# Query features of a fused attention kernel from a second, transposed projection instead of transposed copies

## The chip, the cores and the metric

The kernel runs on one core of a Trainium2 chip, in one launch. The time is device microseconds of that core. Its engines work side by side, each through its own instructions in order: TensorE (PE, with PEld for its weight loads), VectorE (DVE), ScalarE (ACT), GpSimd (POOL), and SyncE (SP), which issues the transfers. Matrix products land in PSUM; the attention turns over six banks of it for all tiles but kv.

## The reference, cut to what matters

Random-feature attention over 4 batches, 8 heads, 576 positions and 64 dimensions with 128 features, and then a mixture of experts on its output (2304 tokens, 512 wide, 8 experts). The change touches `q_p` alone.

```python
def phi(x):
    proj = np.einsum('bhsd,md->bhsm', x, omega)
    sq = np.sum(x * x, axis=-1, keepdims=True) / 2.0
    h = proj - sq
    h = h - np.max(h, axis=-1, keepdims=True)
    return np.exp(h) / np.sqrt(m)
q_p, k_p = (phi(q_s), phi(k_s))
kv = np.einsum('bhsm,bhsd->bhmd', k_p, v)
z = np.sum(k_p, axis=2)
num = np.einsum('bhsm,bhmd->bhsd', q_p, kv)
den = np.einsum('bhsm,bhm->bhs', q_p, z)[..., None] + 1e-06
```

Everything here is fp32. For one position the squared norm and the maximum are the same for all 128 features, so they form one shift per position and head, which is added ahead of the exponential.

## The kernel before

The attention is cut into 36 jobs, 18 of keys and 18 of queries; a job is 128 positions of eight (head, position) slots, kept as two groups g of four. `tick(j)` runs once for each job and overlaps several: for job j it makes the projection (`projections`, tile pp, two banks), the maxima (`maxima`), the shift (`shifts`, tile cn) and the exponentials (`exps`, tile ex); for job j+2 it transposes the input (tile tp, copied to th); for job j-1 it multiplies keys by values (`keys_by_values`, tile kv) or turns the query features; for job j-2 it multiplies query features by that product (`numerators`, tile np) and divides (`quotients`, tile xt). Ticks 5 to 29 take key and query jobs mostly in turn, the last six take queries only.

The features of a query job come out of `exps` with positions on the partitions. `numerators` needs them as stationary operand with features on the partitions. So `query_transposes` sends them through TensorE eight times (tile qp) and `query_copy` brings them back to SBUF on ScalarE (tile qt), one tick after their exponential.

In `projections` and `numerators` the operands cover half of the array: a projection has 64 rows, and the two groups g stand in the upper and the lower half.

The order on each engine is that of the code: the attention's instructions are chained one behind the other in the list `pinned`. Among the ticks `go_on` also advances the work that prepares the experts: sums on GpSimd, casts on ScalarE (tiles wh, xs) and subtractions on VectorE (wl, xs). The experts' products (tiles hx, hz, x, z) follow the attention and fill the rest of the span.

Of the kernel before, what the change touches and what calls it, by code (L numbers as in the profile page):

```python
# [9 lines left out]
F32 = mybir.dt.float32  # L10
F32R = mybir.dt.float32r
AF = mybir.ActivationFunctionType
ALU = mybir.AluOpType
# [9 lines left out]
def moe_attention_kernel(  # L23
# [306 lines left out]
    omt = sc.tile([P, M], F32, name="omt")  # L330

# [113 lines left out]
    def transposed_copy(jb):  # L445

        which, tp = jb[0], tps.pop(jb)
        th = sc.tile([P, 4, P], F32, tag="th", bufs=2, name="th")
        if which == "k":
            nc.scalar.copy(th.rearrange("p a s -> p (a s)"), tp)  # L450
        else:
            nc.vector.tensor_copy(th.rearrange("p a s -> p (a s)"), tp)
        ths[jb] = th

    def projections(jb):

        th = ths.pop(jb)
# [16 lines left out]
    def shifts(jb):  # L474

        cn = sc.tile([P, 8], F32, tag="cn", bufs=4, name="cn")
        nc.vector.tensor_reduce(cn, shift_of(jb), axis=AX.X, op=ALU.add)
        ex = [sc.tile([P, 4, M], F32, tag="ex", bufs=6, name="ex") for _ in range(2)]
        nc.vector.tensor_tensor(
            ex[0], p3s[jb][0], cn[:, 0::2].unsqueeze(2).to_broadcast([P, 4, M]), op=ALU.add  # L480
        )
        cns[jb], exs[jb] = cn, ex

    def exps(jb, g):

        ex = exs[jb][g]
# [7 lines left out]
    tps, ths, p3s, cns, exs, qts, nums = {}, {}, {}, {}, {}, {}, {}  # L494
# [57 lines left out]
    def query_transposes(jb):  # L552

        ex = exs.pop(jb)
        tps = []
        for g in (1, 0):
            tp = bank("qp")
            for i in range(4):
                nc.tensor.transpose(tp[:, i * P : (i + 1) * P], ex[g][:, i, :], ident)
            tps.append((g, tp))  # L560
        return tps

    def query_copy(jb, g, tp):

        t = sc.tile([P, 4, P], F32, tag="qt", bufs=4, name="qt")
        nc.scalar.copy(t.rearrange("p a s -> p (a s)"), tp)
        qts[jb, g] = t
# [443 lines left out]
    def tick(j):  # L1011
# [25 lines left out]
        close()  # L1037
        if now:
# [17 lines left out]
        if job(j - 1, "q"):  # L1056
            for t in query_transposes(job(j - 1)):
                query_copy(job(j - 1), *t)
# [9 lines left out]
        if now:  # L1068
            if it:
                next(it)  # L1070
            exps(now, 1)
        go_on()
# [3 lines left out]
        if now:  # L1076
            exps(now, 0)
# [34 lines left out]
    z = len(jobs)  # L1112
    numerators(jobs[z - 2])
    for g, tp in query_transposes(jobs[z - 1]):
        query_copy(jobs[z - 1], g, tp)
# [143 lines left out]
```

## Time and profile before

| | |
|---|---|
| median of 3 runs | 1576.74 us (1575.73 to 1577.12) |
| the profiled execution | 1575.99 us, of which the span is 1574.2 us |
| TensorE busy | 1561.7 us, 99% of the span |
| TensorE weight loads | 1535.4 us, 98% |
| VectorE, ScalarE, GpSimd busy | 1361.5, 766.2, 277.1 us |
| granted TensorE clock | full speed in all 40 slices |

Attention takes about the first 147 us; the experts take the rest. A matrix product in fp32 stands in the trace as two records (eight projections of a job are 16 MATMUL records), a transpose as one. Ends of matmuls are modelled, so what a group of them takes is read from its start to the start of the next group. That way is used below.

### The profile page before, as it was taken

How to read it: one execution, taken by the hardware profiler on the slowest of the kernel's cores; microseconds unless marked ns; L12 is line 12 of the kernel's file. 1: busy time of each engine (PE TensorE's matmuls, PEld its weight loads, DVE VectorE, ACT ScalarE, POOL GpSimd, SP SyncE). 2: the span in 40 equal slices, each digit the busy share in tenths (PEclk: the TensorE clock that was granted, in tenths of full speed). 3: DMA queues.
4: the chain of work that ended last, by engine and by line, in shares of the span. 5: the costliest groups of instructions: out<-in, count | busy, mean ns of one | idle time of the engine just before them, and what ended most of it. 6: DMA issues, size and time to landing. Idle time of an engine off the chain costs nothing.

```text
span 1574.2 us, 31256 instructions
## 1 busy us (share of the span) xinstructions
PE 1561.7 (99%) x12295; PEld 1535.4 (98%) x12295; DVE 1361.5 (86%) x2573; ACT 766.2 (49%) x1388; POOL 277.1 (18%) x285
## 2 busy tenths in 40 slices
PE   9999999999999999999999999999999999999999
PEld 8887999999999999999999999999999999999998
DVE  7999989898888898888789898889888888989775
ACT  8998654444443444444444443444443444444341
POOL 6665211111010111111011111111110111110000
PEclk9999999999999999999999999999999999999999
DMA  9546866645666666656666666656566666656562
GB/s 227 139 148 259 332 249 223 229 173 214 210 222 215 225 197 216 222 176 216 214 221 212 225 208 212 217 185 225 195 219 212 216 217 208 225 185 212 182 230 92
DMA packets 105730, 330.81 MB, mean 210 GB/s; under 512 B 14704, under 2 KB 43888, under 8 KB 105584
## 3 DMA queue, kind: packets, MB, share of 16 engines
q1 hardware_dynamic: 105296, 328.55, 61.8%
q8 instruction: 98, 1.61, 0.4%
q14 instruction: 48, 0.39, 0.1%
q10 hardware_dynamic: 288, 0.26, 0.0%
HBM read 307.54 MB, written 21.23 MB: 209 GB/s over the span
## 4 chain that ended last, share of the span: by engine, by line
PE 91%; DVE 3%; DMA 3%; ACT 1%; SPq 1%; POOL 1%; issue 0%; DVEq 0%; POOLq 0%; ACTq 0%
PE hx L730 25%; PE x L854 25%; PE hz L730 19%; PE z L854 19%; PE p L938 1%; PE pp L462 1%; DMA xd<-xs 1%; DVE sqs L472 1%; DMA oa<-xd 1%; DMA xs<-xd 1%; DMA k<-in_k_dram 1%; DVE xs L125 0%; PE tp L442 0%; PE np L583 0%; PE kv L499 0%
## 5 line engine op out<-in xcount | busy, mean ns | idle before, releaser
L730 PE MATMUL hx<-xs,wh 128*128 128x384 f32 x1528 | 367.0, 335 | 1.1 <-ACT hn L745 0.8
L730 PE MATMUL hz<-xs,wh 128*128 128x384 f32 x1144 | 282.1, 336 | 0.3 <-DMA xs<-xd 0.3
L730 PEld LDWEIGHTS hx<-xs,wh 128*128 128x128 f32 x1528 | 265.4, 188 | 2.8 <-ACT xs L120 1.4
L235 POOL TENSOR_TENSOR st<-st 128x512 f32<-128x512 f32 x75 | 117.6, 1568 | 613.6 <-DVE wl L269 611.3
L828 ACT ACTIVATE bh<-hr 128x512 fp32r<-128x512 f32 x141 | 89.1, 632 | 237.6 <-PE x L854 230.1
L730 PEld LDWEIGHTS hz<-xs,wh 128*128 128x128 f32 x1144 | 199.8, 188 | 1.5 <-DVE out L888 0.9
L730 PE MATMUL hx<-xs,wl 128*128 128x384 f32 x764 | 200.1, 335 | 0.0
L888 DVE SCALAR_TENSOR_TENSOR out<-x,prob,out 128x256 f32<-128x256 f32 x324 | 153.7, 477 | 52.3 <-PE x L854 50.4
L268 ACT CAST wh<-st 128x512 fp32r<-128x512 f32 x172 | 103.5, 620 | 103.4 <-PE hx L730 52.1
L730 PE MATMUL hz<-xs,wl 128*128 128x384 f32 x572 | 151.8, 335 | 0.0
L825 DVE TENSOR_TENSOR sl<-sm,sh 128x512 fp32r<-128x512 f32 x141 | 112.7, 799 | 44.2 <-ACT sh L823 38.4
L823 ACT CAST sh<-sm 128x512 fp32r<-128x512 f32 x141 | 87.7, 622 | 106.3 <-PE z L854 82.0
L730 PEld LDWEIGHTS hx<-xs,wl 128*128 128x128 f32 x764 | 137.4, 188 | 0.0
L269 DVE TENSOR_TENSOR wl<-st,wh 128x512 fp32r<-128x512 f32 x172 | 123.1, 725 | 9.9 <-ACT wh L268 9.9
L783 DVE SCALAR_TENSOR_TENSOR sm<-hr,sm 128x256 f32<-128x256 f32 x282 | 124.6, 442 | 3.0
L809 ACT CAST sh<-sm 128x512 fp32r<-128x512 f32 x140 | 87.1, 622 | 71.3 <-PE x L854 68.5
L854 PE MATMUL z<-wh,sh 128*128 128x256 f32 x564 | 115.9, 280 | 0.6 <-ACT sh L809 0.5
L854 PE MATMUL x<-wl,sh 128*128 128x256 f32 x564 | 114.5, 280 | 0.0
L854 PE MATMUL z<-wl,sh 128*128 128x256 f32 x564 | 113.9, 280 | 0.0
L854 PE MATMUL x<-wh,sl 128*128 128x256 f32 x564 | 113.6, 279 | 0.0
L791 ACT ACTIVATE ah<-hr 128x256 fp32r<-128x256 f32 x141 | 58.9, 418 | 109.8 <-PE x L854 95.5
L854 PE MATMUL x<-wh,sh 128*128 128x256 f32 x564 | 112.3, 279 | 0.0
(194 smaller groups left out, 3555.6 us busy)
## 6 DMA issues: line engine op xcount, KB each, us to landing
xs<-xd SPq DMA_DIRECT2D x327, 768.0 KB, 4.5
st<-in_moe_w_dram SPq DMA_DIRECT2D x66, 512.0 KB, 4.9
xd<-xs SPq DMA_DIRECT2D x21, 768.0 KB, 5.3
v<-in_v_dram SPq DMA_DIRECT2D x8, 512.0 KB, 7.0
q<-in_q_dram SPq DMA_DIRECT2D x8, 512.0 KB, 7.1
k<-in_k_dram SPq DMA_DIRECT2D x7, 512.0 KB, 7.3
out_dram<-out SPq DMA_DIRECT2D x18, 128.0 KB, 3.9
oa<-xd SPq DMA_DIRECT2D x2, 768.0 KB, 8.9
```

Of the source, the lines that this page charges most:

```text
L235: nc.gpsimd.tensor_tensor(o, a, b, op=op)
L268: nc.scalar.copy(hi, o)
L269: nc.vector.tensor_tensor(lo, o, raw(hi), op=ALU.subtract)
L730: nc.tensor.matmul(pb, lhsT=a[:, k, g * P : (g + 1) * P], rhs=x[:, b, k, :], start=i in (1, 5, 2) and j == 0, stop=j == len(prods) - 1, sk ...
L783: nc.vector.scalar_tensor_tensor(o, in0=a, scalar=0.0, in1=b, op0=ALU.max, op1=op)
L791: nc.scalar.activation(ah, a11, AF.Relu)
L809: nc.scalar.copy(sh, sm)
L823: nc.scalar.copy(sh, sm)
L825: nc.vector.tensor_tensor(sl, sm, raw(sh), op=ALU.subtract)
L828: nc.scalar.activation(bh, a[:, 1:], AF.Relu)
L854: nc.tensor.matmul(pb, lhsT=ops[s][i][a][:, f], rhs=wt[u, 2, i][b][:, f], start=bool(start) and j == 0, stop=j == len(prods) - 1, skip_gro ...
L888: nc.vector.scalar_tensor_tensor(o, in0=pb, scalar=p, in1=o, op0=ALU.mult, op1=ALU.add)
```

## The change

The query job makes no exponential in its own tick. Its shift goes into a zeroed tile cw (`shifts`). In the next tick one transpose on TensorE turns cw, into the job's own first pp bank, and VectorE copies it to a tile ct (`shifts_turned`). `query_features` then projects again with operands exchanged: omega is stationary and the transposed input th moves, 512 columns for each group; eight more products add row i of ct to the 128 columns of slot i, by a stationary operand that repeats one column of the identity. The result is the features' exponent with features on the partitions, and `query_exps` makes two exponentials of 512 columns straight from PSUM into qt. The eight transposes, the two copies, the addition of the shift on VectorE and the five exponentials of a query job go. th is kept a tick longer (4 buffers for 2), and qt shares the buffers of ex (7 for 6 and 4).

```diff
@@ -328,6 +328,10 @@
     sc.tile([P, 1, D], F32, name="om2")
     oms = sc.tile([P, 2, D], F32, name="oms")
     omt = sc.tile([P, M], F32, name="omt")
+    wide = [sc.tile([P, P], F32, name=f"cw{i}") for i in range(2)]
+    turnedc = [sc.tile([P, P], F32, name=f"ct{i}") for i in range(2)]
+    for t in wide:
+        nc.gpsimd.memset(t, 0.0)
 
     def busy(n):
 
@@ -445,7 +449,7 @@
     def transposed_copy(jb):
 
         which, tp = jb[0], tps.pop(jb)
-        th = sc.tile([P, 4, P], F32, tag="th", bufs=2, name="th")
+        th = sc.tile([P, 4, P], F32, tag="th", bufs=4, name="th")
         if which == "k":
             nc.scalar.copy(th.rearrange("p a s -> p (a s)"), tp)
         else:
@@ -454,7 +458,7 @@
 
     def projections(jb):
 
-        th = ths.pop(jb)
+        th = ths[jb] if jb[0] == "q" else ths.pop(jb)
         pp = [bank("pp") for _ in range(2)]
         for i in range(4):
             for g in range(2):
@@ -473,9 +477,18 @@
 
     def shifts(jb):
 
+        if jb[0] == "q":
+            cnw = wide[len(cnws) % 2]
+            cnws.append(cnw)
+            nc.vector.tensor_reduce(
+                cnw.rearrange("p (g c) -> p c g", g=2)[:, :4, :],
+                shift_of(jb).rearrange("p (i g) t -> p i g t", g=2),
+                axis=AX.X, op=ALU.add,
+            )
+            return
         cn = sc.tile([P, 8], F32, tag="cn", bufs=4, name="cn")
         nc.vector.tensor_reduce(cn, shift_of(jb), axis=AX.X, op=ALU.add)
-        ex = [sc.tile([P, 4, M], F32, tag="ex", bufs=6, name="ex") for _ in range(2)]
+        ex = [sc.tile([P, 4, M], F32, tag="ex", bufs=7, name="ex") for _ in range(2)]
         nc.vector.tensor_tensor(
             ex[0], p3s[jb][0], cn[:, 0::2].unsqueeze(2).to_broadcast([P, 4, M]), op=ALU.add
         )
@@ -483,6 +496,8 @@
 
     def exps(jb, g):
 
+        if jb[0] == "q":
+            return
         ex = exs[jb][g]
         if g == 0:
             nc.scalar.activation(ex, ex, AF.Exp)
@@ -491,7 +506,7 @@
         for i in range(4):
             nc.scalar.activation(ex[:, i, :], p3s[jb][1][:, i, :], AF.Exp, bias=c4[:, i : i + 1])
 
-    tps, ths, p3s, cns, exs, qts, nums = {}, {}, {}, {}, {}, {}, {}
+    tps, ths, p3s, cns, exs, qts, nums, cts, qps = {}, {}, {}, {}, {}, {}, {}, {}, {}
 
     def kv_mm(b, h, r, ex, rhs, z, start, stop):
 
@@ -549,22 +564,41 @@
     closing = []
     xts = {}
 
-    def query_transposes(jb):
-
-        ex = exs.pop(jb)
-        tps = []
-        for g in (1, 0):
-            tp = bank("qp")
-            for i in range(4):
-                nc.tensor.transpose(tp[:, i * P : (i + 1) * P], ex[g][:, i, :], ident)
-            tps.append((g, tp))
-        return tps
-
-    def query_copy(jb, g, tp):
-
-        t = sc.tile([P, 4, P], F32, tag="qt", bufs=4, name="qt")
-        nc.scalar.copy(t.rearrange("p a s -> p (a s)"), tp)
-        qts[jb, g] = t
+    cnws = []
+
+    def shifts_turned(jb):
+
+        cp = p3s[jb][0].rearrange("p h m -> p (h m)")[:, :P]
+        nc.tensor.transpose(cp, cnws[-1], ident)
+        ct = turnedc[len(cnws) % 2]
+        nc.vector.tensor_copy(ct, cp)
+        cts[jb] = ct
+        p3s.pop(jb)
+
+    def query_features(jb):
+
+        th, ct = ths.pop(jb), cts.pop(jb)
+        qp = [bank("qp") for _ in range(2)]
+        rows = [slice(g * D, (g + 1) * D) for g in range(2)]
+        for g, r in enumerate(rows):
+            nc.tensor.matmul(
+                qp[g][:, :], lhsT=omt[r], rhs=th[r].rearrange("p a s -> p (a s)"), start=True, stop=False,
+                skip_group_check=True,
+            )
+        for i in range(4):
+            for g, r in enumerate(rows):
+                nc.tensor.matmul(
+                    qp[g][:, i * P : (i + 1) * P], lhsT=ident[r, g * D + i : g * D + i + 1].to_broadcast([D, M]),
+                    rhs=ct[r], start=False, stop=i == 3, skip_group_check=True,
+                )
+        qps[jb] = qp
+
+    def query_exps(jb):
+
+        for g, qp in enumerate(qps.pop(jb)):
+            t = sc.tile([P, 4, P], F32, tag="ex", bufs=7, name="qt")
+            nc.scalar.activation(t.rearrange("p a s -> p (a s)"), qp, AF.Exp)
+            qts[jb, g] = t
 
     def numerators(jb):
 
@@ -1035,6 +1069,9 @@
                 kv_copy(*closed[-1])
 
         close()
+        prev = job(j - 1, "q")
+        if prev:
+            shifts_turned(prev)
         if now:
             projections(now)
             maxima(now, 0)
@@ -1053,9 +1090,8 @@
             next(it)
         if 1 <= j < 3:
             ensure_squares(j - (j < 2))
-        if job(j - 1, "q"):
-            for t in query_transposes(job(j - 1)):
-                query_copy(job(j - 1), *t)
+        if prev:
+            query_features(prev)
         if now:
             if not nxt:
                 go_on()
@@ -1069,12 +1105,13 @@
             if it:
                 next(it)
             exps(now, 1)
+            exps(now, 0)
+        if prev:
+            query_exps(prev)
         go_on()
         for xt, i, t in turned[: 1 if j < 28 else None]:
             turned.pop(0)
             token_copy(token_transposes(xt, i, t), t)
-        if now:
-            exps(now, 0)
         for it in leftover:
             next(it, None)
         leftover.clear()
@@ -1110,9 +1147,10 @@
         tick(i)
         ensure_loads(i + 1)
     z = len(jobs)
+    shifts_turned(jobs[z - 1])
     numerators(jobs[z - 2])
-    for g, tp in query_transposes(jobs[z - 1]):
-        query_copy(jobs[z - 1], g, tp)
+    query_features(jobs[z - 1])
+    query_exps(jobs[z - 1])
     go_on()
     xpss = [token_transposes(*it) for it in turned[:2]]
     quotients(jobs[z - 2])
```

On TensorE, a key tick and the query tick behind it (jobs 9 and 10). Before, from the product of keys and values (kv) that ends the tick ahead:

```order
L499 MATMUL kv<-v_94,ex 64x65 x16
L462 MATMUL pp<-omt,th 128x128 x8
L442 MATMUL tp<-ident,k 128x128 x4
L559 MATMUL qp<-ident,ex 128x128 x8
L462 MATMUL pp<-omt,th 128x128 x8
L442 MATMUL tp<-ident,q 128x128 x4
L583 MATMUL np<-kvs,qt 64x65 x16
```

And in the changed kernel:

```order
L514 MATMUL kv<-v_100,ex 64x65 x16
L572 MATMUL pp<-ident,cw_92 128x128
L466 MATMUL pp<-omt,th 128x128 x8
L446 MATMUL tp<-ident,k 128x128 x4
L584 MATMUL qp<-th,omt 128x512 x2
L590 MATMUL qp<-ct_93,ident 128x128 x8
L466 MATMUL pp<-omt,th 128x128 x8
L446 MATMUL tp<-ident,q 128x128 x4
L617 MATMUL np<-kvs,qt 64x65 x16
```

The transpose of cw stands ahead of the key job's projection, and two products of 512 columns and eight of 128 stand where the eight transposes stood.

On ScalarE, in the same two ticks, from the copies of the earlier query job. Before:

```order
L566 COPY qt<-qp 128x512 x2
L450 COPY th<-tp 128x512
L492 ACTIVATE ex<-pp,cn 128x128 x4
L488 ACTIVATE ex<-ex 128x512
L417 ACTIVATE sq<-q 128x1024
L492 ACTIVATE ex<-pp,cn 128x128 x4
L488 ACTIVATE ex<-ex 128x512
```

And in the changed kernel:

```order
L454 COPY th<-tp 128x512
L507 ACTIVATE ex<-pp,cn 128x128 x4
L503 ACTIVATE ex<-ex 128x512
L600 ACTIVATE qt<-qp 128x512 x2
L421 ACTIVATE sq<-q 128x1024
```

What fills qt stood ahead of the key job's exponentials and now stands behind them; the query job's own five exponentials are gone.

On VectorE, over the same two ticks. Before:

```order
L472 TENSOR_REDUCE sqs<-pp 128x4 x2
L477 TENSOR_REDUCE cn<-sqs 128x8
L479 TENSOR_TENSOR ex<-pp,cn 128x512
L514 TENSOR_TENSOR kvs<-kv,kvs 128x4
L472 TENSOR_REDUCE sqs<-pp 128x4 x2
L477 TENSOR_REDUCE cn<-sqs 128x8
L479 TENSOR_TENSOR ex<-pp,cn 128x512
L452 COPY th<-tp 128x512
```

And in the changed kernel:

```order
L574 COPY ct_94<-pp 128x128
L476 TENSOR_REDUCE sqs<-pp 128x4 x2
L490 TENSOR_REDUCE cn<-sqs 128x8
L492 TENSOR_TENSOR ex<-pp,cn 128x512
L529 TENSOR_TENSOR kvs<-kv,kvs 128x4
L476 TENSOR_REDUCE sqs<-pp 128x4 x2
L483 TENSOR_REDUCE cw_92<-sqs 128x4x2
L456 COPY th<-tp 128x512
```

The query job's addition of 512 columns (ex) goes, a copy of 128 columns (ct) comes in, and the small sum writes cw instead of cn. On GpSimd two memsets of 128 columns come in at the program's start. Behind the attention no engine's order changes.

## Rows read from the trace of the kernel before

**Rows 1.** Busy time and instructions of each engine, and shares of the chain, whole span.

```profile
PE 1561.7 (99%) x12295; PEld 1535.4 (98%) x12295; DVE 1361.5 (86%) x2573; ACT 766.2 (49%) x1388; POOL 277.1 (18%) x285
PE 91%; DVE 3%; DMA 3%; ACT 1%; SPq 1%; POOL 1%; issue 0%; DVEq 0%; POOLq 0%; ACTq 0%
```

**Rows 2.** Chain that ended last, by time: start, length (both us), what.

```profile
14.38 8.32 DMA k<-in_k_dram
...
35.88 0.87 PE qp L559 x8
...
64.45 1.07 ACT qt L566 x2
...
85.38 1.11 DVE xs L125
...
129.88 2.36 POOL v L116
```

**Rows 3.** Busy time by stretch: us, each engine's busy time (instructions), granted clock, DMA.

```profile
28.00:64.00 36.00, 36.00 (x596) 32.44 (x593) 32.01 (x76) 32.80 (x82) 21.08 (x43) 1.00 0.85 210
64.00:85.00 21.00, 20.50 (x328) 17.08 (x328) 17.98 (x42) 20.55 (x50) 14.20 (x25) 1.00 0.01 2
85.00:125.00 40.00, 38.62 (x608) 33.52 (x605) 38.67 (x86) 35.02 (x86) 29.02 (x46) 1.00 0.51 167
125.00:147.00 22.00, 20.69 (x323) 16.16 (x322) 20.94 (x53) 19.84 (x42) 18.90 (x11) 1.00 0.59 231
```

**Rows 4.** Timeline of TensorE, jobs 9 and 10: start, length to the modelled end (us).

```profile
34.13 1.16 PE L462 MATMUL pp<-omt,th 64*128 64x128 f32 x16
35.23 0.66 PE L442 MATMUL tp<-ident,k 128*128 128x128 f32 x4
35.72 1.04 PE L559 MATMUL qp<-ident,ex 128*128 128x128 f32 x8
36.69 1.46 PE L462 MATMUL pp<-omt,th 64*128 64x128 f32 x16
38.08 0.65 PE L442 MATMUL tp<-ident,q 128*128 128x128 f32 x4
38.66 1.15 PE L583 MATMUL np<-kvs,qt 128*64 128x65 f32 x32
...
40.68 1.16 PE L462 MATMUL pp<-omt,th 64*128 64x128 f32 x16
```

**Rows 5.** Timeline of TensorE around the gate's logits (lp), and one later projection.

```profile
79.25 1.50 PE L194 MATMUL lp<-xf,wgs 128*32 128x384 f32 x16
80.68 1.16 PE L462 MATMUL pp<-omt,th 64*128 64x128 f32 x16
...
115.90 1.60 PE L462 MATMUL pp<-omt,th 64*128 64x128 f32 x16
```

**Rows 6.** Groups of instructions, 0 to 200 us: busy us, mean ns, idle before.

```profile
L492 ACT ACTIVATE ex<-pp,cn 128x128 f32<-128x128 f32 x144 | 42.8, 417 | 4.7 <-DVE cn L477 4.3
L488 ACT ACTIVATE ex<-ex 128x512 f32<-128x512 f32 x36 | 25.4, 705 | 0.0
L479 DVE TENSOR_TENSOR ex<-pp,cn 128x512 f32<-128x512 f32 x36 | 24.9, 691 | 2.0
L566 ACT COPY qt<-qp 128x512 f32<-128x512 f32 x36 | 20.1, 617 | 5.6 <-PE qp L559 5.5
L602 DVE TENSOR_TENSOR xt<-np,rd 128x256 f32<-128x256 f32 x36 | 13.6, 418 | 0.6
```

**Rows 7.** Timeline of VectorE and then of ScalarE, job 9's way to its exponentials.

```profile
36.80 0.18 DVE L477 TENSOR_REDUCE cn<-sqs 128x8 f32<-128x24 f32 x1
...
37.79 1.17 ACT L492 ACTIVATE ex<-pp,cn 128x128 f32<-128x128 f32 x4
38.80 0.68 ACT L488 ACTIVATE ex<-ex 128x512 f32<-128x512 f32 x1
39.33 1.10 ACT L417 ACTIVATE sq<-q 128x1024 f32<-128x1024 f32 x1
```

**Rows 8.** Timeline of GpSimd at the start of the span.

```profile
0.86 0.20 POOL L87 MEMSET ones<- 128x128 f32 x1
```

## The prediction

> **What bounds the kernel now.** I read the busy times first. TensorE is busy 99% of the span and carries 91% of the chain that ended last [rows 1]; the change touches only the attention, so the question is what bounds the first 147 us. The chain, read by time, gives the stages [rows 2]. Up to 23 us it runs through transfers. From 28 to 64 us it stays on TensorE, group behind group. Then it passes through ScalarE (64 to 85 us), through VectorE (85 to 125 us), and from 130 us through GpSimd and a transfer, until the experts' first products take over. Next I took busy times by these four stages [rows 3]. TensorE has no idle time in the first, 0.5 us in the second, 1.4 us of 40 in the third and 1.3 us of 22 in the last. So where the chain names ScalarE or VectorE, TensorE is nearly full as well, and a longer TensorE program has little room anywhere. The timeline of one key tick and one query tick shows it piece by piece [rows 4]: one group starts where the other ends.
>
> The clock is granted in full in every stage [rows 3], so each price below holds throughout.
>
> **Prices on TensorE.** Start to start [rows 4]: eight projections of 128 columns take 1.10 us (34.13 to 35.23); four transposes take 0.49 us when transposes follow and 0.58 us when products of another shape follow, so a seam between shapes costs 0.09 us; the eight transposes of query features with their seam take 0.97 us, so 0.11 us each. The projection behind them takes 1.39 us. That is 0.29 us longer than 1.10: it stretches while its second bank waits to be emptied.
>
> What each query job costs after the change:
> - The eight transposes go: 8 x 0.11 = 0.88 us less.
> - Eight products of 128 columns and 64 rows come in. They have the shape of the projections, upper and lower half in turn. Of the 1.10 us some 0.2 are the seams at both ends, so 0.90 us.
> - Two products of 512 columns come in, two records each. No row shows this width. A projection's sixteen records take eight turns of the two halves, 0.90 / 8 = 0.11 us for 128 columns; 512 columns make that 0.45 us a turn, and two turns 0.90 us. The gate's logits (384 columns, four turns of four blocks side by side) take 1.43 us with seams [rows 5], about 0.31 to 0.36 us a turn, which gives 0.82 to 0.96 us for two turns of 512. I take 0.90 us, since the projections have the same 64 rows.
> - The transpose of cw: 0.11 us and one more seam, 0.20 us.
> - Where a projection follows the new block there is no seam behind it; where something else follows (12 of 18 times) there is one, on average 0.06 us.
>
> Together 0.90 + 0.90 + 0.20 + 0.06 - 0.88 = 1.18 us for each query job, 18 x 1.18 = 21.2 us of TensorE.
>
> **What swallows part of it.** Of the 18 features 6, 2, 6 and 4 fall in the four stages.
> - 28 to 64 us: 7.1 us more. Five of the projections behind old transposes are stretched by 0.30 to 0.35 us; the copies they waited for are gone, and the bank is then one whose last reader is early. 7.1 - 1.6 = +5.5 us.
> - 64 to 85 us: 2.4 us more, less 0.5 us idle [rows 3] and 0.8 us of two stretches: +1.1 us.
> - 85 to 125 us: 7.1 us more, less 1.4 us idle [rows 3] and 1.9 us of five stretches (the last of them lasts 1.60 us for 1.16 [rows 4, 5]): +3.8 us.
> - 125 to 147 us: 4.7 us more, less 1.3 us idle [rows 3]. GpSimd is busy 18.9 of these 22 us and in the chain from 129.88 us [rows 2, 3], with sums that start from the tokens of the middle chunk; its end moves by what came before 125 us only, so some of the rest disappears in waits for its transfers. I give that 0.4 us, because the experts' first piece is fed by TensorE and VectorE, not by GpSimd. +3.0 us.
>
> **The other engines.** On ScalarE a query job loses two copies of 0.62 us, one exponential of 0.71 and four of 0.42 us [rows 6], and gains two exponentials from PSUM that lie between the copy's 0.62 and 0.71 us. Even start to start that is over 1 us less. On VectorE the addition of 0.69 us goes and a copy of 128 columns comes in, which lies below the 0.42 us of 256 columns out of PSUM [rows 6]; I take 0.25 us. Both reliefs lie under TensorE, so I price them at nothing. The two memsets cost 0.20 us each by the like one [rows 8]. They precede a chain of transfers [rows 2] and are hidden; uncovered they would cost 0.4 us.
>
> **The new wait.** The exponentials of a query job now stand behind those of the key job on ScalarE, and the numerators wait for them; behind the numerators stand kv and the whole next tick. With the times of job 9 [rows 7]: the shift is ready at 36.98 us; without the old copies ScalarE can begin at about 37.05, needs 1.01 us (37.79 to 38.80) and 0.53 us (38.80 to 39.33), and two more of 0.53 us, so the two halves of qt are there at 39.12 and 39.65 us. TensorE reaches the numerators at 38.66 [rows 4] + 1.18 - 0.20 (the cw transpose is ahead of this tick) - 0.29 = 39.35 us, and their second half 0.5 us later. It is covered, by 0.2 us. That cover fails where VectorE is late with the key job's maxima, and between 85 and 125 us it works 38.67 of 40 us [rows 3]. I add 0.2 us for each of the six features there, 1.2 us. If the cover fails by 0.6 us for each of ten features, it is 6 us. The turn of cw itself waits for VectorE's small sum and stands behind np and kv in the mixed ticks, so I leave it at nothing.
>
> **Sum.** 5.5 + 1.1 + 3.8 + 1.2 + 3.0 = 14.6 us, on the profiled execution's 1575.99 us: 1590.6. That execution lies 0.75 us below the median of the runs shown, so 1591.3; I say 1591.
>
> **A rule weighed.** Weight loads leave more room than products do [rows 3]: 3.6, 3.9, 6.5 and 5.8 us in the four stages, 19.8 us in all. If TensorE were only as full as its weight loads, the 21.2 us would shrink to 1.4 us. The Trainium skill (Trainium Kernel Development and Optimization, Best Practices) says just that the weight loads' busy share and not the matmuls' is to be judged by, because matmuls are pipelined. By that rule the sum would be 1.4 us. I hold against it that the groups of rows 4 start at the next one's heels, and that loads pause at each seam between shapes, where no product can slip in.
>
> **The rivals.**
> - The halves do not run abreast in the products of 512 columns: four turns instead of two, 18 x 0.90 = 16.2 us more, 1607. For it: no row has that width. Against it: sixteen records of 128 columns take 1.10 us, 0.07 us each, where a transpose of 128 columns takes 0.11. 6%.
> - The numerators wait for the late exponentials in most ticks behind 64 us, as priced: 1597. For it: the cover is 0.2 us. Against it: VectorE and ScalarE lose work. 10%.
> - TensorE has the room that its weight loads leave: 1.4 us more, 1578. 5%.
> - Faster: the new block overlaps its neighbours, so that it costs no more time than the transposes with the stretch that they caused, 0.97 + 0.29, about 1.3 us instead of 2.0. From there TensorE stops being the bound. The stretches of the first stage go (1.6 us), ScalarE's relief counts twice between 64 and 85 us (2.9 us by 1.45 each) and VectorE's 0.4 us ten times behind that (4 us): 8.5 us less, 1568. For it: the chain does name ScalarE and VectorE there [rows 2]. Against it: the first stage, where TensorE is never idle. 3%.
>
> **Numbers.** The forecast has 76%: slower by some 14 us. Its own range is 1584 (the block at 0.1 us less, no new wait, the last stage's 3 us hidden behind GpSimd) to 1602 (0.2 us more for each block, and waits as in the second rival). That range takes in the second rival and leaves out the other three (14%) and the forecast's edges, so it stands for the whole. A measurement here can tell a change of about 0.2%, 3 us, from none. Slower than that: the forecast and the first two rivals, 92%. Within it: the third, 5%. Faster: the last, 3%.
>
> **What would show it.** The block from the first product of 512 columns to its end should take 1.8 to 2.0 us, with the two halves' records in pairs; the turn of cw 0.2 us. A key and a query tick in the first stage should go from 6.55 us (34.13 to 40.68 [rows 4]) to about 7.4 us, TensorE without idle time; the projection behind the block should take 1.1 us. VectorE and ScalarE should both show idle time waiting for TensorE between 64 and 125 us. The experts should begin some 14 us later and then take as long as before. I am wrong in size if the products of 512 columns take over 0.5 us a turn, or if numerators wait for qt; wrong in sign if TensorE shows idle time in the first stage.

## The result and the profile after

| | before | after |
|---|---|---|
| time, median of the runs | 1576.24 us (4 runs, 1575.32 to 1577.12) | 1590.13 us (4 runs, 1589.72 to 1590.36) |
| span of the profiled execution | 1574.2 us | 1588.2 us |
| ratio of the times | | 1.0088, 95% interval 1.0070 to 1.0105 |

The change costs 13.9 us in the medians and 14.0 us in the two spans. One execution of a later kernel, the one without the shift products, took 6370.6 us; its ratio leaves it out, and without it its median would be 1581.1 for 1581.19 us. The page of the changed kernel begins like this (busy time and instructions of each engine; shares of the chain), the counterpart of [rows 1]:

```profile
PE 1578.5 (99%) x12529; PEld 1544.1 (97%) x12529; DVE 1355.0 (85%) x2573; ACT 739.9 (47%) x1298; POOL 278.8 (18%) x287
PE 97%; DVE 2%; DMA 1%; ACT 0%; issue 0%; POOL 0%; DVEq 0%; ACTq 0%; POOLq 0%
```

(The engines' names and the columns are those of [rows 1] and [rows 3].) TensorE gained 17 us of busy time, VectorE and ScalarE lost 6.5 and 26 us, and TensorE's share of the chain went from 91% to 97%. Busy times by stage, against [rows 3]:

```profile
28.00:64.00 36.00, 36.00 (x576) 29.52 (x573) 26.27 (x65) 22.00 (x50) 21.20 (x43) 1.00 0.88 209
64.00:85.00 21.00, 21.00 (x363) 17.75 (x359) 16.65 (x40) 15.08 (x31) 12.35 (x24) 1.00 0.01 2
85.00:125.00 40.00, 39.90 (x634) 32.00 (x632) 34.63 (x77) 27.21 (x58) 26.49 (x36) 1.00 0.45 147
125.00:147.00 22.00, 22.00 (x301) 16.55 (x300) 15.10 (x40) 9.17 (x17) 13.28 (x17) 1.00 0.34 121
```

In these 119 us TensorE now idles 0.1 us (3.2 before; 0.8 of that, a wait for xt at the attention's end, is still there, but now falls at 160 us), while its weight loads (second column of busy times) take 95.8 us in all, 99.2 before. The two engines that were relieved wait for it. From 64 to 125 us VectorE waited 1.5 us for projections before; here are its largest wait and one of ScalarE's after (us in total, times, longest):

```profile
DVE sqs L476 <- PE pp L466: 8.1, 11, 1.6
```

```profile
ACT th L454 <- PE tp L446: 5.5, 4, 2.8
```

TensorE's timeline over a key tick and a query tick (start, length to the modelled end), against [rows 4]:

```profile
28.40 0.33 PE L572 MATMUL pp<-ident,cw 128*128 128x128 f32 x1
28.66 1.16 PE L466 MATMUL pp<-omt,th 64*128 64x128 f32 x16
29.75 0.66 PE L446 MATMUL tp<-ident,k 128*128 128x128 f32 x4
30.34 1.13 PE L584 MATMUL qp<-th,omt 64*128 64x512 f32 x4
31.30 1.06 PE L590 MATMUL qp<-ct,ident 64*128 64x128 f32 x16
32.19 1.06 PE L466 MATMUL pp<-omt,th 64*128 64x128 f32 x16
33.18 0.66 PE L446 MATMUL tp<-ident,q 128*128 128x128 f32 x4
33.77 1.16 PE L617 MATMUL np<-kvs,qt 128*64 128x65 f32 x32
34.76 1.10 PE L514 MATMUL kv<-v,ex 128*64 128x65 f32 x32
35.79 0.33 PE L572 MATMUL pp<-ident,cw 128*128 128x128 f32 x1
```

Start to start: the two products of 512 columns 0.96 us, the eight that add the shift 0.89, the turn of cw 0.26, the projection behind the block 0.99 where it was 1.39, the input's transposes ahead of the block 0.59 where they were 0.49. The pair of ticks takes 28.40 to 35.79 = 7.39 us; it took 6.55. The way to the exponentials in the next pair, against [rows 7] (VectorE's sum, ScalarE's key and query exponentials, TensorE's numerators):

```profile
38.64 0.18 DVE L490 TENSOR_REDUCE cn<-sqs 128x8 f32<-128x24 f32 x1
38.91 1.14 ACT L507 ACTIVATE ex<-pp,cn 128x128 f32<-128x128 f32 x4 [0.50 <-DVE cn L490]
39.93 0.65 ACT L503 ACTIVATE ex<-ex 128x512 f32<-128x512 f32 x1
40.45 1.10 ACT L600 ACTIVATE qt<-qp 128x512 f32<-128x512 f32 x2
41.16 1.15 PE L617 MATMUL np<-kvs,qt 128*64 128x65 f32 x32
```

By the prediction's way of counting the first half of qt is there at about 40.45 + 0.53 = 40.98 us, and the numerators begin at 41.16: covered, by 0.2 us. The first of the two exponentials by itself lasts 0.62 us, to 41.07, so the cover is nearer 0.1.

**Where the 14 us arise.** I took the starts of the 36 projections and of the experts' first product (hx) in both timelines; jobs are counted from 0. The changed kernel is 1.07 us behind at job 7, before any query feature (27.59 against 28.66 us); 6.64 at the end of the first stage (68.78 against 75.42); 8.07 at the end of the second (85.66, 93.73); 12.04 at the end of the third (125.43, 137.47); 15.84 at hx (146.84, 162.68). So the stages cost 5.6, 1.4, 4.0 and 3.8 us, with 1.07 us ahead of them. Behind hx some of it is given back: 14.9 us at 196 us, 14.0 at the end.

From job 7 to hx the way is 14.8 us longer. TensorE's idle time on it fell from 3.2 to 0.9 us, and the projections that lasted longer than their like, 4.8 us too long together before, are gone. So TensorE's own program grew by 14.8 + 2.3 + 4.8, some 22 us, and 7.1 us of that took the place of idle time and of stretches.

### The profile page after: what moved, and what is told of

The parts are those of the page before. It is cut to its first block, busy times and chain, and to the rows that moved or that the text cites. A ratio compares the mean times of both kernels' runs of the same rounds, so it can differ in the third digit from the quotient of the medians.

```text
span 1588.2 us, 31605 instructions
## 1 busy us (share of the span) xinstructions
PE 1578.5 (99%) x12529; PEld 1544.1 (97%) x12529; DVE 1355.0 (85%) x2573; ACT 739.9 (47%) x1298; POOL 278.8 (18%) x287
## 4 chain that ended last, share of the span: by engine, by line
PE 97%; DVE 2%; DMA 1%; ACT 0%; issue 0%; POOL 0%; DVEq 0%; ACTq 0%; POOLq 0%
PE hx L764 25%; PE x L888 25%; PE hz L764 19%; PE z L888 19%; PE pp L466 2%; PE np L617 1%; PE kv L514 1%; PE tp L446 1%; PE qp L584 1%; PE p L972 1%; PE qp L590 1%; DMA oa<-xd 1%; PE xp L652 1%; DVE sqs L476 0%; PE pp L572 0%; PE lp L194 0%
## 5 line engine op out<-in xcount | busy, mean ns | idle before, releaser
L235 POOL TENSOR_TENSOR st<-st 128x512 f32<-128x512 f32 x75 | 119.8, 1597 | 613.8 <-DVE wl L269 611.5
L888 PE MATMUL z<-wh,sl 128*128 128x256 f32 x564 | 112.3, 279 | 0.0
```

What stands on the lines that cost most here:

```text
L235: nc.gpsimd.tensor_tensor(o, a, b, op=op)
L888: nc.tensor.matmul(pb, lhsT=ops[s][i][a][:, f], rhs=wt[u, 2, i][b][:, f], start=bool(start) and j == 0, stop=j == len(prods) - 1, skip_gro ...
```

## The experiments

**Does the start, or do the memsets, cost the first microsecond?** In the profile the changed kernel's identity comes 0.2 us later, behind the two memsets, and its first projection 1.2 us later. One kernel moves them away:

```
-    for t in wide:
-        nc.gpsimd.memset(t, 0.0)
...
     nc.gpsimd.memset(vrt[:, :, :1], 1.0)
+    for t in wide:
+        nc.gpsimd.memset(t, 0.0)
```

> The changed kernel with the two memsets of cw moved behind those of v and vr, so that GpSimd makes the identity as early as before. Theory (TensorE has no room from its first instruction on, so a late start is carried to the end): the warm-up transposes start at 1.54 us again instead of 1.75, kv of job 7 at about 26.5 us instead of 27.3, the experts begin 0.8 us earlier, and the time is about 1589.3, 0.8 us under the 1590.1 of the changed kernel. Rival (my prediction's: the transfers up to 23 us set the start anyway and hide the memsets): job 7 and the end stay where they are, 1590.1.

The other adds two memsets to the kernel before, one of a new tile and one of wgs, which is taken earlier:

```
     omt = sc.tile([P, M], F32, name="omt")
+    wgs = sc.tile([P, KD, GC], F32, name="wgs")
+    wide = sc.tile([P, P], F32, name="cw")
+    for t in (wide, wgs):
+        nc.gpsimd.memset(t, 0.0)
```

> The kernel before with nothing but two memsets of 128x128 on GpSimd ahead of the identity, at the place where the change has them. Theory: the start slips by 0.8 us, kv of job 7 starts at about 27.3 us instead of 26.5, and 0.4 to 0.8 us of it is left at the end: 1576.6 to 1577.0. Rival (hidden by the transfers): kv of job 7 at 26.5 us and 1576.2.

Measured: 1589.46 us (1.0083 of before, 1.0070 to 1.0097) and 1577.04 us (1.0002, 0.9993 to 1.0011). With the memsets alone the warm-up starts at 1.74 us, as after the change, but job 7's projection at 27.27, earlier than before's 27.59. The first kernel alone came out as the theory said (0.7 us faster than the changed kernel, job 7 0.9 us earlier); the second contradicts it. So the 0.2 us of the memsets is hidden, as the prediction had it, and my theory here was wrong. Where the microsecond came from shows in TensorE's first rows, first of the changed kernel, then of a kernel with the same memsets (the one without the shift products, below):

```profile
1.75 3.67 PE L340 MATMUL warm<-ident 128*128 128x128 f32 x16 [1.75 <-POOL v L360]
5.21 0.42 PE L346 MATMUL om_ps<-ident,oms 128*128 128x128 f32 x1
5.42 1.06 PE L446 MATMUL tp<-ident,k 128*128 128x128 f32 x4
```

```profile
1.74 3.38 PE L340 MATMUL warm<-ident 128*128 128x128 f32 x16 [1.74 <-POOL v L360]
4.95 0.27 PE L346 MATMUL om_ps<-ident,oms 128*128 128x128 f32 x1
5.06 0.60 PE L446 MATMUL tp<-ident,k 128*128 128x128 f32 x4
```

The first transposes go at 0.2 us each and later ones at 0.11. In the 14 profiled executions of this study the first short one came after 13 to 28 long ones, between 4.4 and 7.5 us, in kernels with and without the memsets. Seven kernels that begin with the same program as the changed one, itself among them, have their first projection anywhere from 6.35 to 7.47 us. It is a matter of the execution, not of the change. The kernel with the memsets behind, which started 0.14 us behind before, lost 5.6, 1.4, 4.0 and 3.8 us in the four stages, the same as the changed kernel.

**Is TensorE's program the time?** Without the eight shift products (the query features lack the shift; the products of 512 columns are then marked as the last of their sum):

```
-        for i in range(4):
-            for g, r in enumerate(rows):
-                nc.tensor.matmul(
-                    qp[g][:, i * P : (i + 1) * P], lhsT=ident[r, g * D + i : g * D + i + 1].to_broadcast([D, M]),
-                    rhs=ct[r], start=False, stop=i == 3, skip_group_check=True,
-                )
```

> The changed kernel without the eight products that add the shift: the query features come out without the shift, all else (first projection, maxima, turn of cw, its copy) stays. The block loses 0.89 us of TensorE and nothing of any other engine. Theory (TensorE's program is the time): 18 x 0.89 = 16 us come off, less some 2 us of waits that show up between 64 and 147 us where ScalarE and VectorE are then nearly as late: 1576, experts some 14 us earlier than in the changed kernel. Rival 1 (TensorE has room; from 64 us on ScalarE and VectorE set the pace): only the six features of 28 to 64 us count, 5 us, 1585. Rival 2 (TensorE is only as full as its weight loads): 2 to 3 us, 1587.

Measured: 1581.19 us (1.0030, 1.0018 to 1.0041), 8.9 us off where 16 us of TensorE went. Its busy times, and the longest wait of TensorE from 28 us on:

```profile
28.00:64.00 36.00, 33.80 (x512) 27.07 (x512) 28.34 (x69) 23.59 (x53) 20.50 (x42) 1.00 0.89 207
```

```profile
PE np L611 <- ACT qt L594: 3.7, 5, 0.9
```

None of the three numbers holds. TensorE now idles 2.2 us in the first stage: the pair of ticks from 35.08 to 42.44 us takes 7.36 us, as long as with the products. Its chain is projection, two maxima and the sum on VectorE, key exponentials, query exponentials, numerators, kv, next projection:

```profile
35.08 1.16 PE L466 MATMUL pp<-omt,th 64*128 64x128 f32 x16
36.27 1.29 DVE L476 TENSOR_REDUCE sqs<-pp 128x4 f32<-128x512 f32 x2 [0.79 <-PE pp L466]
37.67 0.18 DVE L490 TENSOR_REDUCE cn<-sqs 128x8 f32<-128x24 f32 x1
37.95 1.14 ACT L507 ACTIVATE ex<-pp,cn 128x128 f32<-128x128 f32 x4 [0.49 <-DVE cn L490]
...
39.48 1.10 ACT L594 ACTIVATE qt<-qp 128x512 f32<-128x512 f32 x2
40.15 1.17 PE L611 MATMUL np<-kvs,qt 128*64 128x65 f32 x32 [0.78 <-ACT qt L594]
```

With the products, TensorE's program (7.39 us) and this loop are of one length to within 0.2 us in such a pair of ticks. In the pairs that also transpose finished tokens (xp) the loop has more room: 7.9 and 8.2 us here, 8.61 with the products.

In reverse, the kernel before with each query transpose issued twice:

```
-            for i in range(4):
+            for i in (0, 1, 2, 3) * 2:
                 nc.tensor.transpose(tp[:, i * P : (i + 1) * P], ex[g][:, i, :], ident)
```

> The kernel before with each of its eight query transposes issued twice into the same bank: 8 x 0.11 = 0.88 us more of TensorE for each query job, and no work more or less on another engine. Theory: 18 x 0.88 = 15.8 us, less the idle 0.5 + 1.4 + 1.3 us of TensorE between 64 and 147 us: 1576.2 + 12.6 = 1588.8, nearly the changed kernel's time, so that the work which the change takes off ScalarE and VectorE bought next to nothing. Rival 1 (that relief bought several us, so without it the added TensorE time costs more): 1592 or more, since the query copies come 0.88 us later as well. Rival 2 (TensorE has room wherever the chain names ScalarE and VectorE): 6 x 0.88 = 5.3 us of the first stage, 1581.5.

Measured: 1584.16 us (1.0049, 1.0037 to 1.0062), 7.5 us on top for 15.8 us of TensorE. My sum left out that the stretched projections take up added time too. Before, 13 of them between 28 and 125 us last 4.8 us too long; here one does, by 0.3 us. Of the idle 3.2 us 1.1 are left, most of it the wait for xt at the attention's end. So 4.5 + 2.1 = 6.6 us were swallowed, which leaves 15.8 - 6.6 = 9.2 us; from job 7 to hx the profile shows 9.2 us. As after the change some of that is given back behind hx, and 8.2 us are left at the end of the span. ScalarE and VectorE had all their old work, and yet TensorE is nearly full, here from 85 to 125 us:

```profile
85.00:125.00 40.00, 39.73 (x636) 35.08 (x636) 37.04 (x82) 36.27 (x86) 26.77 (x40) 1.00 0.43 146
```

**What is the relief of ScalarE and VectorE worth?** First the relief alone in the kernel before (no shift in the query features):

```
+        if jb[0] == "q":
+            nc.scalar.activation(ex, p3s[jb][g], AF.Exp)
+            return
```

and VectorE's addition is skipped for query jobs.

> The kernel before with only the relief of the change: the query job's exponentials are two instructions of 512 columns straight from PSUM, and VectorE's addition goes; the query features come out without the shift. TensorE's program stays. ScalarE loses some 0.9 us a query job (four of 0.42 against one of 0.71, busy), VectorE 0.69 us. Theory: relief is worth what TensorE waits for the two engines, and no more: 0.5 + 1.4 + 1.3 us idle between 64 and 147 us and some 14 stretched projections of 0.3 us, 7.4 us in all, of which the projections' stretch stays in part since the query copies still follow the transposes: 2 to 5 us off, 1571 to 1574. Rival 1 (relief is worth nothing, as my sum has it for the changed kernel): 1576. Rival 2 (from 64 us on the two engines are the bound): 2 x 1.45 + 10 x 0.4 and the first stage's stretches, 8.5 us off, 1568.

Measured: 1573.30 us (0.9983, 0.9974 to 0.9991), 3.1 us off, within the theory's 2 to 5. By stage: from job 9 (34.13 us) to 64 us it keeps its distance to the kernel before to within 0.04 us, and the five stretched projections there stay as they were. From 68 us to the last projection it gains 2.9 us. Next the relief taken back from the changed kernel, on idle tiles:

```
             cnws.append(cnw)
+            for _ in range(6):
+                nc.vector.tensor_copy(om, om)
...
         if jb[0] == "q":
+            for _ in range(4 if g else 2):
+                nc.scalar.copy(oms, oms)
             return
```

> The changed kernel with the relief taken back: in the tick of a query job ScalarE does six copies of 128 columns and VectorE six of 64 columns more, on tiles that nobody else reads, where the old exponentials and the addition stood (some 1.5 us of ScalarE and 0.6 us of VectorE a query job). TensorE's program stays. Theory (TensorE's program sets the time of the changed kernel, and the relief lies under it): 1590 to 1592. Rival (the relief paid for part of the products): 18 x 0.4 us or more, 1597 and above.

Measured: 1616.34 us (1.0254, 1.0240 to 1.0268). It answers another question than was asked: the six copies on VectorE took 1.25 us together at the least (0.21 us each, twice what I had counted) and up to 4.9 us where GpSimd worked beside them, and they stood ahead of the sum cw, for which TensorE then waited:

```profile
PE pp L576 <- DVE cw L485: 14.4, 8, 3.6
```

In the eight ticks in which the six took about 1.25 us TensorE waited for cw by 0.1 us or less, but for one wait of 0.5; the long waits stand behind the long copies. Behind the two longest (3.6 and 2.9 us) the granted clock also fell to 0.50, from 108 to 114 and from 176 to 182 us, which is part of the 26 us lost. Again with the load behind the sum, `range(2)` behind the sum of cw on VectorE and five copies on ScalarE:

> The changed kernel with the relief taken back once more, but behind the small sum of cw and at the size that was taken off: in the tick of a query job five copies of 128 columns on ScalarE (0.30 us each as run, 1.5 us) and two of 64 columns on VectorE behind cw (0.32 us each, 0.63 us), on tiles that nobody else reads. TensorE's program stays. The first try stood ahead of cw, took 1.9 us of each engine, and TensorE waited 14.4 us in eight waits for cw. Theory (the relief lies under TensorE, what cost time there was the place ahead of cw): 1590 to 1592, no wait for cw over 0.3 us. Rival 1 (the relief paid for part of the products): 1597 and above. Rival 2 (part of it: ScalarE's copies push the query exponentials, and numerators wait for qt): 1593 to 1596.

Measured: 1595.22 us (1.0121, 1.0105 to 1.0136), 5 us more than the changed kernel. From 16 to 98 us every projection starts within 0.05 us of the changed kernel's; all of the loss is behind. There TensorE idles again, on VectorE:

```profile
PE np L621 <- DVE th L456: 0.8, 1, 0.8
...
PE qp L588 <- DVE xt L640: 0.7, 1, 0.7
PE np L621 <- DVE prob L207: 0.6, 1, 0.6
```

The load on VectorE was not what I meant it to be. In most ticks the two copies took 0.33 us, less than the 0.69 - 0.28 = 0.41 us that the change takes off; behind 96 us they took 2.2 to 2.9 us in four ticks and 1.0 in a fifth, beside GpSimd's work:

```profile
142.69 2.70 DVE L489 COPY om<-om 128x64 f32<-128x64 f32 x2
143.49 1.85 POOL L116 TENSOR_TENSOR v<-xf,v 128x768 f32<-128x768 f32 x1
```

The first time lost follows the first such tick (96.66 to 99.6 us), and the waits for th (at 146.0 us) and for prob (at 152.6) stand right behind two others. The work that the change took off, an addition out of PSUM, took 0.69 us in every tick of the kernel before. So the 5 us is the price of these copies, not of the relief. Last, the five copies on ScalarE alone (the two of VectorE left out):

> The changed kernel with only ScalarE's relief taken back (five copies of 128 columns, 1.5 us, in the tick of a query job), and VectorE as changed. With both taken back the time was 1595.2, all of it lost behind 93 us, in waits of TensorE that end on VectorE (for th, prob and xt, 2.4 us). Theory (behind 93 us it is VectorE's relief that counts, ScalarE's is worth nothing): 1590 to 1591. Rival 1 (ScalarE's relief counts, since VectorE's copies and additions wait for it): 1594 to 1595. Rival 2 (each has its part): 1592 to 1593.

Measured: 1589.94 us (1.0084, 1.0071 to 1.0098), with ScalarE loaded nearly as before the change (35.02 us in this stretch) and TensorE full:

```profile
85.00:125.00 40.00, 39.97 (x636) 31.94 (x635) 34.80 (x80) 34.14 (x84) 26.14 (x36) 1.00 0.45 147
```

ScalarE's relief is worth nothing, with VectorE relieved; VectorE's, as far as 0.33 us a tick can show, is worth nothing up to 96 us. What VectorE's is worth behind that stays open: no run put a load of the right size there. The doubled transposes, with VectorE's old work in place, filled 1.1 of TensorE's 1.4 idle us between 85 and 125 us, which speaks for little.

**Does the new order of exponentials cost anything?** The query job's ahead of the key job's again:

```
+        if prev:
+            query_exps(prev)
         if now:
             exps(now, 1)
             exps(now, 0)
-        if prev:
-            query_exps(prev)
```

> The changed kernel with the query job's exponentials ahead of those of the key job on ScalarE, as the kernel before had its copies. Nothing is added or removed. Theory (the numerators' new wait costs next to nothing, since their exponentials are there just in time, and TensorE is the bound either way): 1589 to 1591. Rival 1 (my 1.2 us between 85 and 125 us were there): 1588.5 to 1589. Rival 2 (the key job's exponentials, now 1.06 us later, hold up kv): 1592 and above.

Measured: 1592.94 us (1.0105, 1.0091 to 1.0119), 2.8 us slower than the changed kernel. That is rival 2: kv waits for the key job's exponentials (the changed kernel waits 0.2 us for them in all):

```profile
PE kv L514 <- ACT ex L503: 2.2, 5, 1.3
```

The 1.3 us stand ahead of 14 us, where the kernel before waits as long; from 26 us on it is 0.8 us in four waits. The rest shows as stretch: the numerators ahead of kv take 1.31 and 1.36 us in the first two pairs of ticks, 0.98 in the changed kernel, and these pairs take 7.8 us for 7.4.

The same order in the kernel without the shift products:

> The kernel without the eight shift products (query features without the shift), and with the query job's exponentials ahead of the key job's on ScalarE. Without the products alone the time was 1581.2, and the numerators waited 3.7 us for qt. Theory (that wait is what kept the full 16 us from coming back): it goes, and 3 to 4 us with it: 1577 to 1578. Rival 1 (the wait only moves: kv waits for the key job's exponentials, 1.06 us later): 1581 or more. Rival 2 (VectorE's maxima are what TensorE waits for): 1580 to 1581, with idle time of TensorE that ends on VectorE.

Measured: 1578.71 us (1.0015, 1.0006 to 1.0024), 2.5 us off: between theory and rival 1. The numerators' 3.7 us went, and from 28 us on kv waits 0.8 us in four waits instead. So which order is better depends on how long TensorE's block is.

**Can the transposed projection win at all?** Without the shift altogether: the eight products, cw, the first projection, maxima and squares of query jobs are left out, and the query features are the exponentials of the second projection.

```
     def projections(jb):
+        if jb[0] == "q":
+            return
...
-    sq_todo = [it for it in need if it[1] != "v"]
+    sq_todo = [it for it in need if it[1] == "k"]
```

> The query features from the transposed projection alone, as the exponential of q times omega: the shift by square and maximum is left out (it stands in numerator and denominator alike, and only the 1e-6 sees it), and with it the first projection, the maxima, the squares, cw, its turn and the eight products of every query job. Against the kernel without the shift products (1581.2) TensorE loses 1.10 + 0.26 us a query job, VectorE two maxima of 0.69, cw and ct, ScalarE and GpSimd the squares. Theory (TensorE's program sets the time of the attention in all these kernels): 18 x 1.36 = 24.5 us off, 1557, with TensorE still busy 95% of 28 to 125 us. Rival 1 (the transfers of q, k and v up to 64 us set the pace once TensorE is shorter): the first 6 features bring nothing, 1565. Rival 2 (the key jobs' ScalarE and VectorE work is what TensorE waits for): half of it, 1569.

Measured: 1570.94 us (0.9968, 0.9955 to 0.9980), nearest to rival 2. The numerators waited for qt, 11.9 us in ten waits:

```profile
PE np L604 <- ACT qt L587: 11.9, 10, 1.9
```

With the query exponentials first:

> The kernel that leaves the shift out of the query features (1570.9), with the query job's exponentials ahead of the key job's on ScalarE; these wait for nothing but the products of 512 columns. There the numerators waited 11.9 us in ten waits for qt, because these exponentials stood behind the key job's, which wait for two maxima and cn on VectorE. Theory (that queue place is what holds the kernel without the shift): most of the wait goes, kv waits for the key job's exponentials by 0.2 us or so a tick instead: 8 to 10 us off, 1561 to 1563. Rival (the wait moves to kv in full, as the key job's exponentials come 1.06 us later): 1570 to 1572.

Measured: 1567.93 us (0.9941, 0.9928 to 0.9955), the fastest kernel here, but 3.0 us off and not 8. Its profiled execution is the slowest of its five (1571.40 us; the others took 1566.09 to 1568.43), so its trace shows more loss than its median has. One turn of its loop in the first stage:

```profile
36.45 1.16 PE L464 MATMUL pp<-omt,th 64*128 64x128 f32 x16
...
37.64 1.29 DVE L476 TENSOR_REDUCE sqs<-pp 128x4 f32<-128x512 f32 x2 [1.90 <-PE pp L464]
39.04 0.18 DVE L483 TENSOR_REDUCE cn<-sqs 128x8 f32<-128x24 f32 x1
...
39.35 1.09 ACT L587 ACTIVATE qt<-qp 128x512 f32<-128x512 f32 x2 [0.53 <-PE qp L577]
...
40.32 1.15 ACT L500 ACTIVATE ex<-pp,cn 128x128 f32<-128x128 f32 x4
...
41.32 0.67 ACT L496 ACTIVATE ex<-ex 128x512 f32<-128x512 f32 x1
...
42.04 1.15 PE L507 MATMUL kv<-v,ex 128*64 128x65 f32 x32 [0.86 <-ACT ex L496]
```

From this projection to the next (43.12 us) it is 6.67 us, no less than the 6.55 of the full kernel before. TensorE idles in between. What sets the tick is the way from a projection over TensorE's own next groups (the input's transposes and the products of 512 columns) to ScalarE, which then does the query and the key exponentials without a pause, and to kv. VectorE is not on it: cn is there at 39.22 us, and the key job's exponentials, which need it, begin at 40.32, right behind the query job's, which waited for TensorE. I had expected kv to wait 0.2 us; it waits 0.86. And of the 9.4 us by which this execution is ahead of the kernel before at 164 us, 4.5 are lost again by 173 us, 3.0 of them where TensorE waits for a transfer to the experts:

```profile
PE hz L751 <- DMA oa<-xd: 3.0, 1, 3.0
```

The other 1.5 us follow that wait, with the granted clock at 0.50 from 164 to 166 us and 0.69 in the next two.

## Why the prediction came out as it did

Predicted 1591 us, measured 1590.1. The mechanism was right: TensorE was full, its program grew by some 22 us by the rows (predicted 21.2), and what idle time and stretches did not swallow came out at the experts' first product. That the total came so close is partly luck, since several errors of 1 to 2 us in the parts cancel. Point by point:

- **Prices on TensorE: right.** The block takes 0.96 + 0.89 = 1.85 us (predicted 1.8), the turn of cw 0.26 (0.20), the projection behind the block 0.99 (1.10), the pair of ticks 7.39 us (about 7.4). The seam ahead of the block, 0.10 us a feature (0.59 for 0.49), is missing in the sum. Two products of 512 columns on each half take 0.96 us together and not 1.8, so the halves run in pairs and the first rival falls.
- **First two stages: right.** 5.6 and 1.4 us, predicted 5.5 and 1.1. The doubled transposes bear out the way they were worked out, that idle time and stretches swallow added TensorE time before the end moves: 9.2 us by that way and 9.2 measured up to hx, though single stages there are up to 1 us off.
- **85 to 125 us: near in size, by a sum of which two terms were wrong.** Measured 4.0, predicted 3.8 + 1.2. The 3.8 leaves out a sixth stretch (the projection at 108.69 us, 0.5 us beyond its idle time) and so should have been 3.3; that it is close to the 4.0 is luck. The 1.2 us for the numerators' new wait measured nothing: the cover that I worked out holds, and TensorE idles 0.1 us ahead of numerators between 28 and 147 us (the second rival falls), and it is thin, since the kernel with a block 0.89 us shorter waits up to 0.9 us there. I had the sign of the order as a whole wrong: the key job's exponentials first save 2.8 us.
- **"Both reliefs at nothing": right for ScalarE, and for VectorE up to 96 us; open for VectorE behind that.** The run that put VectorE's work back lost its 5 us behind copies that took several times the work they stood for. Of the 1.4 us of idle time that I subtracted, at least 1.1 ended on VectorE before, so part of the relief may be counted there under another name; the doubled transposes filled most of that time without the relief.
- **125 us to the experts: 3.8 us, predicted 3.0.** Of the idle 1.3 us only 0.5 were swallowed: the wait of 0.8 us for xt stands at the end of the attention in both kernels (144.7 and 160.5 us). That GpSimd hid anything (the 0.4 us) no run shows.
- **"The experts then take as long as before": wrong by 1.8 us.** 0.9 us come back by 196 us, and 0.9 us later. Of the first, before's TensorE waited 0.3 us for xs at hx, where after there is no such wait; for the rest I have no cause, and the kernel with two memsets alone, 0.4 us ahead at hx and 1.2 us behind at the end, suggests that spans drift by as much by themselves. With the 1.07 us of this execution's start the two errors nearly cancel in the total.
- **Memsets at nothing: right,** by the two kernels on them.
- **The weighed rule: the measurement speaks against it.** Weight loads were 90% busy in the first stage before the change and 82% after it, and yet TensorE had no idle time there and the stage grew by 5.6 us: the sum by the rule was 1.4 us, the change cost 13.9. The Trainium skill's sentence on judging by the weight loads' busy share (Trainium Kernel Development and Optimization, Best Practices) speaks of the distance to roofline; read as room for more work, as I read it, it does not hold for these fp32 groups with a seam every microsecond. The third rival falls.
- **The faster rival** needed TensorE to stop being the bound. The block had to cost 1.3 us; it costs 1.85 and 0.26 for cw, less 0.4 at the projection behind it.
- **Slips in the sums.** The second rival's 1597 adds its 6 us to a forecast that already has 1.2 us of the same wait; 1596 is meant. By the terms given for the range its ends are 1585 and some 1600, not 1584 and 1602.

## What to carry to other kernels

A hand-ordered schedule can have two bounds of nearly one length: here TensorE's program (7.39 us a pair of ticks after the change) and a loop of waits through VectorE and ScalarE (7.36 us in the kernel without the shift products). Then added work counts in full once idle time and stretches are used up (15.8 us added, 9.2 more up to the experts), and removed work comes back only as far as the loop lets it (16 us removed, 8.9 back), so a price from one side says little of the other; before trading work between engines, walk the loop from one projection to the next and compare it with the busiest engine's sum. Count as slack what the busy time hides too, such as groups that last longer than their like.

## What was not expected of the hardware

- A short wait of TensorE can be followed by a lower clock. In both kernels that leave the shift out, TensorE waited 0.7 us for the exponentials ahead of kv near 27 us. In the one with the query exponentials first (27.14 us) it had been busy 1.29 of the 2 us from 26 to 28 us, and was granted the lower level (0.50 of full, 1.2 GHz) from 28 to 30 us, and a group of kv took 1.91 us instead of 1.15, the projection behind it 1.96 instead of 1.16:

```profile
26.00:28.00 2.00, 1.29 (x34) 1.16 (x30) 0.00 (x0) 1.08 (x4) 1.69 (x5) 0.82 0.87 239
28.00:30.00 2.00, 2.00 (x29) 1.88 (x27) 0.00 (x0) 0.00 (x0) 0.47 (x3) 0.50 0.88 235
```

So 1.6 us of what a shorter TensorE program had saved went back at once. The wait alone does not decide it: later waits of up to 1.9 us, the numerators' in the kernel with the key exponentials first, left the granted clock at 1.00. What does decide it these runs do not show.

- The first transposes of an execution ran at 0.2 us, twice their later 0.11, for 13 to 28 of them, a spread of some 1.3 us in where the first projection starts (6.2 to 7.5 us), although the granted clock of these stretches reads 1.00. In one of the 14 executions (28 of them) all transposes ahead of the first projection were long.

- A VectorE copy can last as long as the GpSimd instruction beside it. In the kernel with the load behind cw, copies of 64 columns from SBUF to SBUF took 0.2 us in most ticks, but ten took 0.47 to 1.78 us, and each of the ten ended 0.05 us after a GpSimd instruction that had begun before it. A load of copies put in to stand for other work has to be checked in the trace before its price is believed.
